# Linear attention and a two-layer sine network: longer runs of q, the key decay moved to v, two more DMA transposes, smaller filler matmuls and a new scheduler

## The chip, the cores and the metric

The kernel runs on one core of one Trainium2 chip. The metric is the device time in microseconds. Of a core's five engines, TensorE (PE) multiplies matrices into the eight banks of PSUM, VectorE (DVE), ScalarE (ACT) and GpSimd (POOL) work on vectors, and SyncE (SP) issues transfers. Each engine executes its own instructions in order; semaphores order the engines among each other.

## The reference

Inputs are q, k and v of 4 batches, 8 heads, 768 tokens and 64 channels, one decay `lam` per head, and the network's weights, all float32.

```python
for b in range(nb):                      # blocks of 64 tokens
    intra = einsum('bhic,bhjc->bhij', qb, kb) * Dmask     # lam ** (i - j) for i >= j
    intra = einsum('bhij,bhjd->bhid', intra, vb)
    inter = einsum('bhid,bhde->bhie', qb * lam ** (pos + 1), kv_state)
    out[:, :, sl] = intra + inter
    kv_state = lam ** 64 * kv_state + einsum('bhsd,bhse->bhde', kb * lam ** (63 - pos), vb)
x = out as (3072 tokens, 512)
h = x @ w_in                             # 512 -> 2048
g = h + sin(alpha * h) ** 2 / (alpha + 1e-9)
return g @ w_out                         # 2048 -> 512
```

Because the decay is a power, it splits: q of token i is multiplied by lam to the i, and something of token j by lam to the minus j; the mask is then only zeros and ones.

## The kernel before

**Tiles.** The kernel uses blocks of 128 tokens: 24 blocks, six per batch. Four blocks make a chunk of 512 tokens, the unit in which the network works; there are six chunks. A block takes these steps. Its q, k and v are loaded (`load_q` for two blocks at once, `load_kv`), 256 KB each of k and v and 512 KB of q for two blocks. `scale_block` multiplies q by its decay (L464, on POOL, one instruction per half of the heads), k by the inverse decay (L471, on POOL, for blocks 0 and 1 on DVE), both to bf16, and casts v to bf16 (L473, on ACT, from block 12 on ACT or POOL). `piece_Q` and `piece_T` transpose q and k on PE (L506, L488) and copy them out of PSUM (L511, L493); from block `TD` = 12 on `piece_T` issues one DMA transpose on SP instead (L479). `part_S` multiplies k and q to scores (L543) and masks them on DVE (L552). `part_Z` adds the block's k and v to the running state (L568), copied out at L583 (`Zc`) or, from block `SD` = 12 on, at L578 (`Zd`). `part_O` multiplies state and q (L616, or L603) and masked scores and v (L623) and copies the sum to `xT` (L632).

**The network.** A first-layer unit, `unit_A`, makes 128 of the 2048 columns for a chunk: four matmuls of 512 columns (L671), the sine on ACT (L681), its square on POOL or ACT (L686, or L685 when it is on ACT), and on DVE the sum to `gT` (L688). `unit_A2` makes 256 columns for half a chunk with eight matmuls of 256 columns (L705, L715, L719 or L720, L723); it needs only two blocks of the chunk. A second-layer unit, `unit_B`, is four matmuls (L736) over a quarter of the 2048 rows for 128 tokens; after the fourth the result is copied to `osb` on ACT (L749) and stored (L751). The four `osb` buffers are used in turn.

**Transfers.** The first quarter of `w_in` is loaded by SP as float32 (`ws`) and cast on DVE (L391); the other three quarters (`load_w1`) and the four of `w_out` (`load_w2`) are loaded and cast by POOL's queue (L342 is the one line of all loads). k, v and q lie in rings of buffers, so a load also waits until the buffer's last reader is done.

**Order.** The calls to `op` record work with what it reads and writes, and a duration. `_Plan._order` then plays the work through with those durations and gives each engine a fixed order: PE and SP from lists in which PE may look 40 ahead, the other engines whatever can start first, ties by the place in the recording less a `lead`. An operation with several engines goes to the one that would finish it first. `_transfers` estimates landings; `_settle` repeats both up to eight times. Until the first unit is ready, `spin` fills waits of PE with matmuls whose result nobody reads (L829, 512 columns). The order is fixed when the program is built: on the chip an engine waits for its next instruction even if a later one could run.

A q load of blocks 0 to 3 takes, for each partition and head, two tokens (512 bytes):

```python
for lo, hi in ((0, 4), (4, H)) if s < 4 else ((0, H),):
    ... q[b, lo:hi, n * BL:(n + 2) * BL, :].rearrange("h (p t) d -> p h (t d)", t=2)
```

Of the kernel before, what the change touches and what calls it, by code (L numbers as in the profile page):

```python
# [13 lines left out]
class _Op:  # L14


    def __init__(self, eng, emit, dur, reads, writes, dma, after, issue, lat, runs=64):
        self.eng, self.emit, self.dur = eng, emit, dur
        self.given = eng
        self.issue, self.lat, self.runs = issue, lat, runs  # L20
        self.lead = 0
# [11 lines left out]
class _Plan:  # L33

    AHEAD = {"PE": 40, "SP": 1}
    SLACK = 0.3  # L40
    EARLY = 0.0, 0.0

    LAT = 0.2
# [10 lines left out]
    def op(self, eng, emit, dur, reads=(), writes=(), dma=None, after=(), issue=0.4, lat=2.6, runs=64):  # L54
# [14 lines left out]
        o.deps.discard(o)  # L69
        o.lead = self.lead  # L70
# [4 lines left out]
    def _transfers(order):  # L75
# [5 lines left out]
        left = {e: [[o.start + 0.8, o.runs, o.dur / o.runs, o] for o in sorted(q, key=lambda o: o.start)]  # L81
# [19 lines left out]
    def _settle(self):  # L101

        filler, lands, best = self.filler, {}, None
        for _ in range(8):
            self.filler = filler
            for o in self.ops:
                o.eng, o.start, o.done = o.given, None, None
            order = self._order(lands)
            new = self._transfers(order)
            off = sum(abs(t - o.done) for o, t in new.items())  # L110
            state = [(o, o.eng, o.start, o.done) for o in order]
            if best is None or off < best[0]:
                best = off, order, state
            lands = new
# [4 lines left out]
    def _order(self, lands):  # L119
        index = {o: i - o.lead for i, o in enumerate(self.ops)}  # L120
        left = {}
        for o in self.ops:
            left.setdefault(o.eng if isinstance(o.eng, str) else "any", []).append(o)
        fixed = {e: left.pop(e, []) for e in ("PE", "SP")}
        free = [o for e in left for o in left[e]]
        clock = {e: 0.8 for e in ("PE", "SP", "ACT", "DVE", "POOL")}
        wire = 0.0
        port = 0.0
        order = []

        def ready(o):
            t = 0.0
            for d in o.deps:
                if d.done is None:
                    return None
                t = max(t, d.done + (0.0 if d.eng == o.eng else self.LAT))
            return t

        while fixed["PE"] or fixed["SP"] or free:
            best = None  # L140
            for e in ("PE", "SP"):
                can = []
                for o in fixed[e][:self.AHEAD[e]]:
# [9 lines left out]
            for o in free:  # L153
                r = ready(o)
                if r is None:
                    continue
# [773 lines left out]
```

## Time and profile before

| | us |
|---|---|
| median of three runs (lowest, highest) | 223.09 (222.61, 224.41) |
| the profiled execution | 223.52 |
| its span, first to last instruction | 221.4 |
| start of the first layer (first L705) | 19.89 |
| start of the unit that needs the second quarter of `w_in` | 23.72 |
| end of the stretch in which first and second layer alternate | 204 |

| stretch, us | PE busy | DVE | ACT | POOL | GB/s |
|---|---|---|---|---|---|
| 0 to 20 | 14.36 | 13.83 | 10.26 | 12.43 | 219 |
| 20 to 52 | 29.52 | 17.64 | 20.35 | 17.37 | 214 |
| 52 to 86 | 31.97 | 25.95 | 28.18 | 25.73 | 235 |
| 86 to 204 | 117.93 | 63.85 | 93.37 | 32.48 | 108 |
| 204 to 222 | 14.82 | 1.29 | 3.78 | 1.04 | 74 |

Busy is the time in which an engine executes an instruction; issuing a transfer and waiting count as idle. Matmuls overlap, so a single one shows 0.37 us where four in a row take 0.86. The landing of a transfer is the last of its sixteen semaphore counts.

### The profile page before, as it was taken

Reading aid. Unit: us, or ns where it says so; the run is one execution under the profiler, and the core shown is the slowest. Engines: PE = TensorE matmul, PEld = TensorE weight load, DVE = VectorE, ACT = ScalarE, POOL = GpSimd, SP = SyncE. Lnnn points to the kernel's source line nnn. Section 1 sums busy time; section 2 is a strip of 40 time slices with the busy share of each in tenths; the row PEclk is TensorE's granted clock in tenths of the full one; section 3 lists DMA queues with packets and bytes.
Section 4 is the critical chain, followed back from the end, with each engine's and each line's share of the span. In section 5 each row is a group of like instructions: output and inputs, shape, how many; then the busy total and the mean of one; then the engine's idle time right before and its main releaser. Section 6 shows DMA issues by size and latency. Waiting matters only on the chain.

```text
span 221.4 us, 4062 instructions
## 1 busy us (share of the span) xinstructions
PE 208.6 (94%) x1645; PEld 110.7 (50%) x1645; DVE 122.6 (55%) x184; ACT 155.9 (70%) x277; POOL 89.1 (40%) x100
## 2 busy tenths in 40 slices
PE   3889987899898999999999999999999999999995
PEld 1446433456575785545445444545545444444444
DVE  4687775354777887667655455645465544445100
ACT  3735994347697997788788887877788677778211
POOL 4386763454978776863576103011001011110100
DMA  5999999999999999999999752110110011101112
GB/s 131 236 232 271 206 214 208 217 235 237 233 245 275 242 191 245 219 254 189 276 240 245 155 112 33 47 50 0 47 50 21 26 47 50 47 0 49 75 70 95
DMA packets 83651, 33.31 MB, mean 150 GB/s; under 512 B 63520, under 2 KB 80688, under 8 KB 83632
## 3 DMA queue, kind: packets, MB, share of 16 engines
q1 hardware_dynamic: 76880, 24.25, 53.6%
q0 software_dynamic: 3696, 3.67, 9.9%
q10 hardware_dynamic: 3056, 5.13, 6.4%
q8 instruction: 13, 0.21, 0.4%
q14 instruction: 6, 0.05, 0.1%
HBM read 27.28 MB, written 6.29 MB: 152 GB/s over the span
## 4 chain that ended last, share of the span: by engine, by line
PE 63%; DMA 24%; POOL 4%; SPq 4%; ACT 2%; DVE 1%; issue 1%
PE bank L736 32%; PE bank L671 24%; DMA k<-in_k_dram 10%; DMA q<-in_q_dram 5%; DMA v<-in_v_dram 4%; DMA w<-in_moe_w_in_dram 4%; SPq L342 4%; PE bank L705 3%; PE bank L623 2%; PE bank L543 2%; POOL qk L471 1%; POOL qk L464 1%; PE bank L603 1%; POOL u L720 1%; DVE gT L723 1%
## 5 line engine op out<-in xcount | busy, mean ns | idle before, releaser
L736 PE MATMUL bank<-w,gT 128*128 128x512 bf16 (+1 forms) x400 | 94.8, 371 | 0.0
L688 DVE SCALAR_TENSOR_TENSOR gT<-u,rinv,bank 128x512 bf16<-128x512 bf16 x74 | 54.6, 746 | 51.7 <-ACT u L685 34.2
L671 PE MATMUL bank<-xT,w 128*128 128x512 bf16 x296 | 74.2, 379 | 0.6 <-DVE gT L688 0.6
L681 ACT ACTIVATE t<-bank,alpha 128x512 bf16<-128x512 f32 x74 | 50.6, 686 | 24.1 <-PE bank L671 24.0
L736 PEld LDWEIGHTS bank<-w,gT 128*128 128x128 bf16 x400 | 37.7, 98 | 39.6
L686 POOL TENSOR_TENSOR u<-t 128x512 bf16<-128x512 bf16 x19 | 19.7, 1040 | 80.7 <-ACT t L681 79.7
L671 PEld LDWEIGHTS bank<-xT,w 128*128 128x128 bf16 x296 | 28.5, 98 | 34.9 <-DVE gT L688 1.1
L685 ACT ACTIVATE u<-t 128x512 bf16<-128x512 bf16 x55 | 34.4, 629 | 1.8 <-DVE gT L723 0.3
L552 DVE TENSOR_TENSOR Sm<-bank,mask 128x1024 bf16<-128x1024 f32 x24 | 29.2, 1222 | 10.3 <-PE bank L568 7.7
L464 POOL TENSOR_TENSOR qk<-q,Lq 128x512 bf16<-128x512 f32 x24 | 24.5, 1044 | 21.7 <-DMA q<-in_q_dram 18.1
L471 POOL TENSOR_TENSOR qk<-k,Lk 128x512 bf16<-128x512 f32 x22 | 22.9, 1044 | 7.2 <-DMA k<-in_k_dram 7.0
L749 ACT COPY osb<-bank 128x512 f32<-128x512 f32 (+1 forms) x25 | 14.2, 569 | 14.8 <-PE bank L736 14.8
L705 PE MATMUL bank<-xT,w 128*128 128x256 bf16 x176 | 22.3, 273 | 2.0 <-DVE gT L723 2.0
L723 DVE SCALAR_TENSOR_TENSOR gT<-u,rinv,bank 128x256 bf16<-128x256 bf16 x44 | 19.1, 476 | 7.2 <-POOL u L720 4.1
L715 ACT ACTIVATE t<-bank,alpha 128x256 bf16<-128x256 f32 x44 | 18.5, 471 | 3.3 <-PE bank L705 3.1
L705 PEld LDWEIGHTS bank<-xT,w 128*128 128x128 bf16 x176 | 16.2, 98 | 5.5 <-DVE gT L723 3.0
L473 ACT CAST v<-v 128x512 bf16<-128x512 f32 x18 | 11.0, 615 | 7.6 <-DMA v<-in_v_dram 7.6
L632 ACT CAST xT<-bank 128x512 bf16<-128x512 f32 (+1 forms) x18 | 12.9, 716 | 2.8 <-PE bank L568 1.6
L720 POOL TENSOR_TENSOR u<-t 128x512 bf16<-128x512 bf16 x11 | 11.3, 1039 | 4.7 <-ACT t L715 4.6
L543 PE MATMUL bank<-qkT 64*128 64x128 bf16 x192 | 9.8, 226 | 0.2 <-DVE qkT L493 0.2
L623 PE MATMUL bank<-Sm,v 128*64 128x128 bf16 x192 | 9.9, 225 | 0.0
L829 PE MATMUL bank<-mask,ident 128*128 128x512 bf16 x12 | 5.7, 564 | 3.7 <-DVE mask L429 3.7
(55 smaller groups left out, 111.4 us busy)
## 6 DMA issues: line engine op xcount, KB each, us to landing
k<-in_k_dram SPq DMA_DIRECT2D x24, 256.0 KB, 5.5
v<-in_v_dram SPq DMA_DIRECT2D x24, 256.0 KB, 5.5
q<-in_q_dram SPq DMA_DIRECT2D x10, 512.0 KB, 5.5
out_dram<-osb ACTq DMA_DIRECT2D x19, 256.0 KB, 2.0
w<-in_moe_w_out_dram POOLq DMA_DIRECT2D x4, 512.0 KB, 13.1
w<-in_moe_w_in_dram POOLq DMA_DIRECT2D x3, 512.0 KB, 9.0
q<-in_q_dram SPq DMA_DIRECT2D x4, 256.0 KB, 4.6
ws<-in_moe_w_in_dram SPq DMA_DIRECT2D x2, 512.0 KB, 5.4
```

The lines of the kernel that those rows point to most:

```text
L464: lambda e, a=a: e.tensor_tensor(qk2[:, j:j + 2, 4 * a:4 * a + 4, :], q32[jq][:, 4 * a:4 * a + 4, :, :].rearrange("p h t d -> p t h d"), b ...
L471: lambda e: e.tensor_tensor(qk2[:, j, H:2 * H, :], k32[jl][:, :, :], lk, ALU.mult), 0.7 if s in (0,1) else 1.05,
L552: op("DVE", lambda e: e.tensor_tensor(Sm[s % 2][:, :, :], banks[:, 512 * b0:512 * b0 + 1024].rearrange("p (c i) -> p c i", i=128), mask[:, ...
L671: ins = e.matmul(ps[hb][:, c0:c1], w1[:, kc, 128 * m:128 * (m + 1)], xT[x][:, kc, c0:c1], start=(kc == 0 and c0 == lo), stop=(kc == NKC - ...
L681: op("ACT", lambda e: e.activation(t16[ju][:, w], ps[hb][:, w], ACTF.Sin, scale=alpha[:, m:m + 1]), 0.69 * f, [bank(hb), "alpha"], [("t16" ...
L685: lambda e: (e.activation(u16[ju][:, w], t16[ju][:, w], ACTF.Square) if e is nc.scalar else e.tensor_tensor(u16[ju][:, w], t16[ju][:, w], ...
L686: e.tensor_tensor(u16[ju][:, w], t16[ju][:, w], t16[ju][:, w], ALU.mult)), 0,
L688: op("DVE", lambda e: e.scalar_tensor_tensor(out=gT[g][:, m, w], in0=u16[ju][:, w], scalar=rinv[:, m:m + 1], in1=ps[hb][:, w], op0=ALU.mul ...
L705: ins = e.matmul(ps[hb][:, 256 * i:256 * i + 256], w1[:, kc, 128 * (m + i):128 * (m + i + 1)], xT[x][:, kc, lo:lo + 256], start=(kc == 0 a ...
L715: op("ACT", lambda e, i=i: e.activation(t16[ju][:, 256 * i:256 * i + 256], ps[hb][:, 256 * i:256 * i + 256], ACTF.Sin, scale=alpha[:, m + ...
L723: op("DVE", lambda e, i=i: e.scalar_tensor_tensor(out=gT[g][:, m + i, lo:lo + 256], in0=u16[ju][:, 256 * i:256 * i + 256], scalar=rinv[:, ...
L736: ins = e.matmul(ps[ob][:, w], gT[g][:, m, 128 * s4:128 * (s4 + 1)], w2[:, m, w], start=(m == 0), stop=(m == NM - 1),)
```

## The change

- q of blocks 0 to 3 is loaded in two transfers of 512 KB, each four heads of 512 tokens, in runs of four tokens (1 KB). A block of scores then takes its 128 queries from four transposed tiles with 32 columns each, and a mask of its own; `queries` gives the tiles. q of these blocks is scaled on DVE, in four instructions. The decay table gets four more rows.
- The inverse decay is multiplied into v (POOL, L524) and k is only cast (ACT, from block 12 on ACT or POOL, L521).
- `TD` goes from 12 to 10: blocks 10 and 11 are transposed by DMA.
- The fillers multiply a tile of ones, `idle`, and have 256 columns; they need only that tile.
- The mask is one 128x128 tile read eight times, instead of a 128x1024 tile; there are two, one for blocks 0 to 3.
- The loads of `w_in` and `w_out` wait for v of block 2 instead of k of block 3; the second quarter of `w_in` has a lead of 400. `prep` loads two blocks ahead from block 8 instead of 10. Chunk 0's stores are recorded after `prep(13)`.
- The scheduler: for each engine the candidates within a window of the soonest are taken by priority; the time between two dependent operations is by engine; most durations change; and `MOVES` shifts the priority of listed stretches of the recording. Engines that have a choice can choose otherwise, and every engine's order differs.

In the built programs POOL has 15 squares for 30, ACT 81 for 66; PE has 80 single transposes for 96 and 68 fillers for 12; SP has 14 DMA transposes for 12.

```diff
-    AHEAD = {"PE": 40, "SP": 1}
-    SLACK = 0.3
-    LAT = 0.2
+    AHEAD = 40
+    WINDOW = {"PE": 0.3, "ACT": 0.1, "DVE": 0.1, "POOL": 0.1}
+    PIPE = {"ACT": 0.11, "DVE": 0.09, "POOL": 0.045, "PE": 0.0}
+    HOP = {"PE": 0.055, "ACT": 0.035, "DVE": 0.035, "POOL": 0.075, "SP": 0.1}
+    DRAIN = 0.085
+    MOVES = (
+        (501, 30, "all", 10), (454, 30, "all", -180), (471, 1, "all", 140), (439, 10, "all", -70),
...
+        prio = {o: i - o.lead for i, o in enumerate(self.ops)}
+        for at, width, kind, by in self.MOVES:
+            for o in self.ops[at:at + width]:
+                if (kind == "all" and o.given != "SP") or o.given == kind or (kind == "any" and not isinstance(o.given, str)):
+                    prio[o] += by
...
+                soon = min(x[0] for x in c) + self.WINDOW.get(e, 0.0)
+                x = min((x for x in c if x[0] <= soon), key=lambda x: (x[1], num[x[2]]))
...
-    TD = 12
+    TD = 10
...
+                if s < 4:
+                    for a in range(2):
+                        last["q32", s] = load(
+                            q32[:, a, :, :, :].rearrange("p (h x) t d -> p h (x t d)", x=2),
+                            q[0, 4 * a:4 * a + 4, 0:4 * BL, :].rearrange("h (p t) d -> p h (t d)", t=4),
...
-                ported(op("DVE" if s in (0,1) else "POOL",
-                   lambda e: e.tensor_tensor(qk2[:, j, H:2 * H, :], k32[jl][:, :, :], lk, ALU.mult), 0.7 if s in (0,1) else 1.05,
-                   [("k32", jl), "Lk"], [("k2", j)]))
-                op((("ACT", 0.62, 0.0), ("POOL", 1.05, 0.3)) if s > 11 else "ACT", lambda e: (e.copy if e is nc.scalar else e.tensor_copy)(v2[j][:, :, :], v32[jl][:, :, :]), 0.62,
-                   [("v32", jl)], [("v2", j)])
+                op((("ACT", 0.62, 0.0), ("POOL", 0.62, 0.3)) if s > 11 else "ACT", lambda e: (e.copy if e is nc.scalar else e.tensor_copy)(
+                    qk2[:, j, H:2 * H, :], k32[jl][:, :, :]), 0.62, [("k32", jl)], [("k2", j)])
+                ported(op("POOL",
+                   lambda e: e.tensor_tensor(v2[j][:, :, :], v32[jl][:, :, :], lk, ALU.mult), 1.05,
+                   [("v32", jl), "Lk"], [("v2", j)]))
...
+            def queries(s):
+                nq = 4 if s < 4 else 2
+                w = BL // nq
+                return s % RT // nq * nq, nq, slice(w * (s % nq), w * (s % nq) + w)
...
-                    for ahead in range(s + 2, min(s + 3, NBLK)) if s >= 10 else ():
+                    for ahead in range(s + 2, min(s + 3, NBLK)) if s >= 8 else ():
...
             for i in range(1, 4):
-                load_w1(i, [last["k32", 3]])
+                P.lead = 400 if i <= 1 else 0
+                load_w1(i, [last["v32", 2]])
...
-                    ins = e.matmul(ps[0][:, :], ident[:, :], mask[:, 0:4, :].rearrange("p a b -> p (a b)"))
+                    ins = e.matmul(ps[0][:, 0:256], idle[:, 0:128], idle[:, :])
...
-            load_pair(10)
...
-            for st in stores:
-                if st is not None:
-                    st("SP")
             pieces = pieces_of(8, None, False) + pieces_of(10, 9, False)
...
             prep(12)
             prep(13)
+            for st in stores:
+                if st is not None:
+                    st("SP")
```

## The prediction

> **What bounds the kernel now.** I read first the page's busy shares and its costliest groups, then the waits of TensorE after 20 us, the stage table, the timelines of TensorE and ScalarE around each idle time, and the DMA issues with their landings.
>
> ```profile
> PE 208.6 (94%) x1645; PEld 110.7 (50%) x1645; DVE 122.6 (55%) x184; ACT 155.9 (70%) x277; POOL 89.1 (40%) x100
> L736 PE MATMUL bank<-w,gT 128*128 128x512 bf16 (+1 forms) x400 | 94.8, 371 | 0.0
> ```
>
> The line under the shares is the second layer; TensorE is the bound. From 19.89 us, when the first L705 starts, to 218.86, when the last result is copied out, TensorE stands still 4.5 us. Its own waits in that stretch:
>
> ```profile
> PE bank L705 <- DVE gT L723: 2.0, 3, 1.0
> PE bank L506 <- POOL qk L464: 1.7, 1, 1.7
> PE bank L671 <- DVE gT L688: 0.6, 1, 0.6
> PE bank L488 <- POOL qk L471: 0.2, 1, 0.2
> ```
>
> (total us, times, longest.) In the timeline they lie at 30.5 (0.57), 39.3 (1.72), 43.6 (0.18), 59.3 (0.82), 69.1 (1.01) and 85.4 (0.19); after 86 there is nothing to win but work itself. A unit of four 512-column matmuls takes 0.86 us there, full rate.
>
> What stands behind the idle times is mostly memory traffic:
>
> ```profile
> 17.00:19.00 2.00, 1.83 (x34) 1.00 1.11 344
> 21.00:29.00 8.00, 8.00 (x49) 1.00 1.24 206
> 30.00:36.00 6.00, 5.49 (x26) 1.00 1.19 217
> ```
>
> (stretch, length, TensorE busy, clock, DMA share, GB/s.) The DMA engines are full from 4 to 42 us. q of blocks 4 and 5 is issued at 25.87, lands 12.3 us later at 38.1, and TensorE waits for its scaling until 39.3. The wait at 59.3 is another kind:
>
> ```profile
> 54.65 0.82 ACT L715 ACTIVATE t<-bank,alpha 128x256 bf16<-128x256 f32 x2
> 57.16 0.62 ACT L473 CAST v<-v 128x512 bf16<-128x512 f32 x1 [1.69 <-DMA v<-in_v_dram]
> 57.68 0.63 ACT L719 ACTIVATE u<-t 128x512 bf16<-128x512 bf16 x1
> ```
>
> ScalarE executes in order; its cast of v waits 1.69 us for a landing, the square behind it comes late, and TensorE finds no free bank for 0.82.
>
> **The head.** Blocks 0 to 3 load q, k, v in 256 KB pieces. k and v pieces land 1.17 us apart (7.11, 8.29, 9.46, 10.62), q pieces 0.90 to 0.95 (512-byte packets), so 1 MB of q costs about 3.7. The 512 KB pieces of w (1 KB packets) land 1.40 apart (18.71 and 20.11). With q in 1 KB runs, 1 MB costs 2.8 to 3.1. The first pieces fall in the ramp (100 to 140 KB per us until 4 us), where I take nothing: for the second half that is 1.85 for 1.4 to 1.55, so 0.3 to 0.9 in all, 0.5 taken. All later landings move up so much: k of block 3 from 14.86 to 14.35, v of block 2 from 16.08 to 15.55, the w pieces from 18.71 and 20.11 to 18.2 and 19.6.
>
> The row is 287 GB/s at 10 to 11 us, 512-byte packets, against 344 at 17 to 19, 1 KB packets. The Trainium skill ("DMA: Bandwidth & Descriptors", Specifications) puts line rate at 512 bytes and up; by it the longer runs give nothing, the landings stay, and the sum below would be 0.5 smaller. The trace disagrees.
>
> From k3 the path was: scaling on POOL 1.04, transposes, copy 0.42, scores 0.33, mask 1.18, output, w cast 0.68, first layer at 19.89. Now ScalarE casts k (0.62) and may do the copy (0.59): 14.35+0.62+0.25+0.59+0.33 = 16.2, two hops of 0.1, mask until 17.6. The w cast then waits for its landing at 18.2, and the first layer starts at about 19.0, 0.9 earlier. v is scaled on POOL (1.04 for 0.62), which has the path's slack: v3 lands 16.7; behind v2 and a weight issue of 0.94 it is ready at about 18.3.
>
> But TensorE then needs quarter 1 of w_in. It issued at 15.91 and landed at 23.30; the fifth unit began at 23.72, just covered. In the changed order it is issued on v2's landing, about 15.55, and k of block 4 is issued before it without a wait, so 256 KB run beside it. Queues share by packet: at 30 to 36 us the packet records have 137 KB per us of weights (1 KB, 96 ns each) beside 70 of q (512 bytes), two to one. Beside 256-byte packets (24 ns) they get 96/(96+24) = 80% of 201, so 512 KB take 3.2 us instead of 2.55: landing 23.3 + 0.65 - 0.4 to -0.6 = 23.4. TensorE would be there at 19.0+3.83 = 22.85: it stands about 0.5, and of the 0.9 there is 0.3 left (bounds -0.3 and +0.9). The fillers are 68 of 256 columns for 12 of 512; a run too long delays the step behind it by at most nine times 0.11, and the 0.5 covers that.
>
> **20 to 52 us.** The changed TensorE order has seven second-layer units ahead of the q transposes of block 4, where there were four. From 23.4: nine units 7.8, a bank wait as before (ScalarE takes two more squares of 0.63 in this layer; 0.5 to 1.0, 0.8 taken), then ten more units (8.6) and 0.3 for quarter 2 of w_out (due about 39.0): 40.9. q, issued when quarter 2 of w_in lands (26.5 for 25.87), is there at about 38.8, its two scalings end at 40.9: no wait worth naming. k of block 4 is long there, k5 (44.0 for 44.20) too. So idle 1.1 for 2.5: 1.4 gained (0.4 to 2.0).
>
> **52 to 86 us.** Here idle is 2.0, with ScalarE busy 28.2 of 34. k lands 1.0 to 1.2 before v of the same block (56.15 and 57.14), and it is k that ScalarE now waits for; v's wait moves to POOL. Against that ScalarE takes over squares: 81 of them for 66, 9.5 us in all, some of it here. I take half of the 2.0: 1.0 (-1.0 to 2.0).
>
> **Transposes of blocks 10 and 11.** On TensorE they were 0.45 for q and two of 0.23: 0.9 off the bound, and 0.69+2*0.42 of copies. On SP they add two issues of 2 to 3 us (L479 rows: 2.73, 2.35), in front of the loads of block 14 and of chunk 0's four stores, which move behind block 13's transpose: loads of 12 and 13 from 62.0 (5.8, as now), two transposes (5.1), then what took 72.0 to 83.2, at most 11.2: stores at 81.5 to 84.1 instead of 62.6, landed 4.0 later, at 85.5 to 88.1. ScalarE's next output copy needs that buffer at about 84.5; behind it wait one sine and one square, while TensorE has four second-layer units (3.5 us) that need neither. Cover until about 88.5: nothing charged; past it each us late costs a us. The loads behind have slack: k and v of blocks 22 and 23 land by 124 us, used after 160.
>
> Masks (128x128, read with stride 0) and constants are off the path; the multiply keeps its shape, 1.22.
>
> **Sum** against the profiled execution, 223.52 (221.4 span and 2.1 around it): 0.3+1.4+1.0+0.9 = 3.6 off, 219.9. That execution is 0.43 above the median of 223.09, so 219.5.
>
> **Rivals.**
> *Landings rule all of it.* If block 4 to 11's data set the pace, only the stream's 0.5 and the transposes' 0.9 count: 1.4, 221.7. For it: a DMA share of 1.0 and more until 120 us. Against: the waits at 30.5, 59.3 and 69.1 end with VectorE. Chance 0.20.
>
> *All idle goes.* 0.9+4.5+0.9 = 6.3: 216.8. For it: no single resource is full from 52 to 86. Chance 0.08.
>
> *ScalarE's k casts, the slower side.* Nine k casts (blocks 5 to 13) stand between sines; the nine v casts waited 6.9 us in all from 20 to 86. If each cost TensorE the 0.82 of 59.3, that is 7.4 against 4.6 gained with the old idle gone: 225.9. Slower than before from six of nine, by over 1% only with all. For it: the added squares leave ScalarE less slack. Against: k lands first. Chance 0.08.
>
> *The clock falls back in the head.* Half rate shows in fillers: 0.61 us for one at 11.76, 0.38 at 15.13; TensorE needed from 3.66 to 12.3 to get fast. If the small fillers don't hold it, up to 8.6 us of first layer go at half rate, 0 to 4.3 lost; at 2, 221.5. By the Trainium skill ("TensorE: Matmul & The Clock Gate", Part 4: PE-mode transpose) transposes do not count as activity, which speaks for it; the rows from 13 to 19 us stayed fast with transposes among them. Chance 0.04.
>
> The forecast itself has 0.60 and 218.0 to 220.8. About 1% (2.2 us) is what a measurement can tell here, so bounds 220.9 and 225.3. Faster: 0.60+0.08 = 0.68; same: 0.20+0.04 and the milder k casts 0.02 = 0.26; slower 0.06. The range takes the forecast, most of the landings rival and part of the all-gone case: 217.5 to 222.5.
>
> **What will show it.** First layer at about 19.0, a wait of TensorE for the w_in DMA of about 0.5, fifth unit near 23.4; idle from there to 52 near 1.1; no wait behind a cast at 59; 40 L506 and 40 L488 transposes for 48 each; stores landing before 88. Wrong if quarter 1 lands after 24.5, if ScalarE idles over 1 us on k landings several times, or if TensorE waits after 86.

## The result, and the profile after

The changed kernel takes 225.97 us (median of 20 executions, 223.97 to 228.15), the kernel before 223.74 beside it (20, 222.61 to 225.14). The ratio is 1.0072, with a 95% interval of 1.0049 to 1.0096: a little slower, where 219.5 was predicted. Ratios, here and below, leave out executions over 1.5% above the fastest of the same kernel (four of these 20); the medians keep them. The profiled execution of after took 225.33, with a span of 223.6.

The busy shares and the costliest group of after, in the columns of before:

```profile
PE 212.9 (95%) x1685; PEld 115.1 (51%) x1685; DVE 122.2 (55%) x185; ACT 162.5 (73%) x295; POOL 72.0 (32%) x84
L795 PE MATMUL bank<-w,gT 128*128 128x512 bf16 (+1 forms) x400 | 95.3, 373 | 0.0
```

TensorE is busy 4.3 us longer than before, although 16 transposes left it. Part of that is fillers, part is real matmuls at half clock, as will be seen. Its five largest waits after 20 us (total us, times, longest):

```profile
PE bank L662 <- DVE gT L747: 2.1, 1, 2.1
PE bank L601 <- DVE gT L782: 0.9, 1, 0.9
PE bank L601 <- DMA qkT<-qk: 0.7, 1, 0.7
PE bank L764 <- ACT t L774: 0.6, 1, 0.6
PE bank L662 <- DMA qkT<-qk: 0.6, 1, 0.6
```

Of the idle times of before, the 1.72 at 39.3 is gone and the 0.57 at 30.5 is 0.41, at 31.26. One wait is new: 2.1 us in front of the matmuls of state and q (L662) of blocks 15 and 16. In TensorE's timeline of after (start, us, engine, line, operation, and in brackets the idle time before it with its releaser):

```profile
108.10 1.03 PE L795 MATMUL bank<-w,gT 128*128 128x512 bf16 x4
111.23 0.38 PE L662 MATMUL bank<-qkT,Zd 128*128 128x128 bf16 x4 [2.11 <-DVE gT L747]
112.34 1.72 PE L730 MATMUL bank<-xT,w 128*128 128x512 bf16 x4
113.85 1.91 PE L795 MATMUL bank<-w,gT 128*128 128x512 bf16 x4
```

The releaser named there, a sum on VectorE, is misleading. The group also needs the DMA transpose of block 17, since q comes in runs of two tokens for two blocks, so that the scores of block 16 read the transposed tiles of blocks 16 and 17. That transpose landed at 111.14, 0.09 us before the group starts. In before it landed at 105.94, 5.5 us ahead of the same group:

```profile
111.47 0.39 PE L603 MATMUL bank<-qkT,Zd 128*128 128x128 bf16 x4
```

In after, units of four matmuls right behind the wait take 1.7 to 1.9 us where they took 0.86 to 1.04. The stage table of after (stretch, length, TensorE busy, clock, DMA share, GB/s) has the reason:

```profile
109.00:111.00 2.00, 0.12 (x1) 1.00 0.47 94
112.00:113.00 1.00, 1.00 (x18) 0.78 1.20 319
113.00:114.00 1.00, 1.00 (x4) 0.50 1.35 228
114.00:115.00 1.00, 1.00 (x4) 0.50 1.34 217
115.00:116.00 1.00, 1.00 (x4) 0.51 1.19 225
116.00:117.00 1.00, 1.00 (x6) 1.00 1.01 230
```

After 2.11 us without matmuls the granted clock (the share of TensorE's full clock) fell to 0.50 for over three us: 112 to 116 hold 4 x 1.00 us of busy time at 0.78, 0.50, 0.50 and 0.51, which is 0.22 + 0.50 + 0.50 + 0.49 = 1.7 us of lost work. The Trainium skill ("TensorE: Matmul & The Clock Gate", Why this matters for your kernels) tells to avoid idle gaps of over about 3 us. By it this gap would have been free of that price; the measurement differs.

Why the transpose is late stands in SyncE's timeline (start, us in which it issues):

```profile
69.60 4.14 SPq L530 DMA_TRANSPOSE qkT<-qk  x2
...
83.63 2.08 SPq L810 DMA_DIRECT2D out_dram<-osb  x4
...
88.84 4.96 SPq L530 DMA_TRANSPOSE qkT<-qk  x1
95.41 1.96 SPq L530 DMA_TRANSPOSE qkT<-qk  x1
100.21 2.63 SPq L530 DMA_TRANSPOSE qkT<-qk  x1
104.13 4.73 SPq L530 DMA_TRANSPOSE qkT<-qk  x1
```

Here SyncE issues without a pause from 69.6 to 108.9. The first line is the two added transposes; the four stores of chunk 0 now follow at 83.63 instead of 62.6; the last line is block 17's, whose issue took 4.73. The casts and scalings that it reads were done at 98.45, 5.7 us before. The same one in before was issued at 101.68, in 1.91:

```profile
95.75 2.88 SPq L479 DMA_TRANSPOSE qkT<-qk  x1
101.68 1.91 SPq L479 DMA_TRANSPOSE qkT<-qk  x1
```

So its landing is 5.2 us later: 2.45 because its issue starts later and 2.8 because its issue takes longer. In before SyncE issues without a pause too, from 76.8 on, and block 17's transpose stood there 6.4 us behind its inputs (done at 95.31): the queue that got the added work was already full at that place.

### The profile page after: what moved, and what is told of

Its sections match the earlier page's. It is cut to its first block, busy times and chain, and to the rows that moved or that the text cites. A ratio compares the mean times of both kernels' runs of the same rounds, so it can differ in the third digit from the quotient of the medians.

```text
span 223.6 us, 4144 instructions
## 1 busy us (share of the span) xinstructions
PE 212.9 (95%) x1685; PEld 115.1 (51%) x1685; DVE 122.2 (55%) x185; ACT 162.5 (73%) x295; POOL 72.0 (32%) x84
## 4 chain that ended last, share of the span: by engine, by line
PE 78%; DMA 6%; DVE 5%; POOL 4%; ACT 3%; issue 2%; SPq 1%; ACTq 0%; POOLq 0%
PE bank L795 37%; PE bank L730 25%; PE bank L764 5%; DMA qkT<-qk 4%; PE bank L682 3%; PE bank L601 3%; DMA alphaT<-in_moe_alpha_dram 2%; DVE Sm L610 2%; POOL u L745 1%; PE bank L662 1%; PE bank L557 1%; DVE xT L691 1%; ACT t L774 1%; POOL u L779 1%; POOL qk L516 1%
## 5 line engine op out<-in xcount | busy, mean ns | idle before, releaser
L730 PE MATMUL bank<-xT,w 128*128 128x512 bf16 x296 | 75.0, 383 | 0.5 <-DVE gT L747 0.4
L740 ACT ACTIVATE t<-bank,alpha 128x512 bf16<-128x512 f32 x74 | 50.0, 686 | 16.7 <-PE bank L730 15.9
L744 ACT ACTIVATE u<-t 128x512 bf16<-128x512 bf16 x66 | 41.6, 630 | 2.2 <-DVE gT L782 0.2
L524 POOL TENSOR_TENSOR v<-v,Lk 128x512 bf16<-128x512 f32 x24 | 25.0, 1044 | 21.6 <-DMA v<-in_v_dram 20.2
L516 POOL TENSOR_TENSOR qk<-q,Lq 128x512 bf16<-128x512 f32 x20 | 20.5, 1044 | 20.7 <-DMA q<-in_q_dram 20.7
L521 ACT CAST qk<-k 128x512 bf16<-128x512 f32 x19 | 11.8, 620 | 2.9 <-DMA k<-in_k_dram 2.8
L890 PE MATMUL bank<-idle 128*128 128x256 bf16 x68 | 12.1, 320 | 1.3 <-DVE idle L455 1.3
L691 ACT CAST xT<-bank 128x512 bf16<-128x512 f32 (+1 forms) x16 | 11.7, 729 | 1.8 <-PE bank L682 1.2
L778 ACT ACTIVATE u<-t 128x512 bf16<-128x512 bf16 x15 | 9.5, 641 | 0.2
L779 POOL TENSOR_TENSOR u<-t 128x512 bf16<-128x512 bf16 x7 | 7.3, 1040 | 7.2 <-ACT t L774 7.2
```

What stands on the lines that cost most here:

```text
L516: lambda e, a=a: e.tensor_tensor(qk2[:, j:j + 2, 4 * a:4 * a + 4, :], q32[:, jq, 4 * a:4 * a + 4, :, :].rearrange("p h t d -> p t h d"), b ...
L524: lambda e: e.tensor_tensor(v2[j][:, :, :], v32[jl][:, :, :], lk, ALU.mult), 1.05,
L730: ins = e.matmul(ps[hb][:, c0:c1], w1[:, kc, 128 * m:128 * (m + 1)], xT[x][:, kc, c0:c1], start=(kc == 0 and c0 == lo), stop=(kc == NKC - ...
L740: op("ACT", lambda e: e.activation(t16[ju][:, w], ps[hb][:, w], ACTF.Sin, scale=alpha[:, m:m + 1]), 0.69 if hi - lo == TCH else 0.475, [ba ...
L744: lambda e: (e.activation(u16[ju][:, w], t16[ju][:, w], ACTF.Square) if e is nc.scalar else e.tensor_tensor(u16[ju][:, w], t16[ju][:, w], ...
```

## The experiments

Except where told, each kernel is after with its instruction order kept as built and only the listed edit: `_edit` runs once the planner has settled the order, `_put` moves an instruction, `at` is its planned time. Three figures compare them. *T17* is the landing of block 17's transpose (105.94 in before, 111.14 in after). *Rest* is the time from the start of the L662 group of blocks 15 and 16 to TensorE's end. *Ratio* is against runs of before on the same chip, with its 95% interval; after has 1.0072 [1.0049, 1.0096]. T17 and rest come from one profile each, and two profiles of one kernel differed by 2.1 us in T17, so a ratio weighs more than one landing. In six of the profiles the first loads landed about 2 us late; it is said where that matters.

**The stores, to ScalarE's queue.**

```diff
+    acts = [o for o in order if o.eng == "ACT"]
+    for row in range(4):
+        st = _find(order, "store", row)
+        copy = next(d for d in st.deps if d.dma is None)
+        st.eng = "ACT"
+        _put(order, st, acts[acts.index(copy) + 2], True)
```

> The four stores of chunk 0 are issued by ScalarE, each two instructions behind its copy, in place of SP between the transposes of blocks 13 and 14; every other instruction stays where it was. Queue theory (SP issues without a pause from 69.6 to 108.9 us in the changed kernel, so the 2.08 us of the stores delay all that follows): the transpose of block 14 is issued at about 86.8 in place of 88.84, that of block 17 lands at about 109 in place of 111.14, TensorE's waits of 0.55 us at 99.79 and 2.11 us at 111.23 go, and with them the stretch of half clock behind the second (1.65 us): about 4.2 us less than 225.33, ratio to before near 0.988. Order theory (TensorE's new order asks for block 16 about 9 us earlier than the old one, and the transposes wait for their own inputs): no gain, ratio near 1.007. Contention theory (the transfers themselves are slow beside the stores): the bytes stay, the wait at 111 shrinks by less than 1 us.

Ratio 1.0027 [0.9995, 1.006], 224.08 us. T17 108.58, group at 111.82: no wait for the transpose any more, but TensorE now waited 1.52 at 78.63 and 1.50 at 89.23. T17 is 2.6 us earlier without these four issues on SyncE, but freeing the queue alone gains little: the waits moved.

**The wait filled with matmuls nobody reads.**

```diff
+    g = next(o for o in order if o.eng == "PE" and any(d.tag == ("T", 17) for d in o.deps))
...
+    def spins(h):
+        for _ in range(19):
+            ins = plan.spin1(h)
+        return ins
+    f = _Op("PE", spins, 2.0, (), (), None, (), 0, 0)
...
+    order.insert(order.index(g), f)
```

> 19 unused matmuls of 128x256 are put on TensorE ahead of the group that waits for the transpose of block 17, where it stood idle for 2.11 us; nothing else moves. Clock theory (the idle stretch itself costs 1.65 us more, since the granted clock was 0.50 for the 3 us behind it): the wait stays about as long but filled, the clock stays above 0.9 from 111 to 116, and the time falls by about 1.65 us to 223.7, ratio near 1.000. If the drop comes by itself and only happens to lie there: no change, ratio near 1.007.

Ratio 1.0053 [1.0017, 1.0089], 225.14 us. Its stage table:

```profile
110.00:112.00 2.00, 2.00 (x17) 1.00 0.51 89
112.00:113.00 1.00, 1.00 (x13) 1.00 0.52 146
113.00:114.00 1.00, 0.94 (x27) 1.00 1.11 328
114.00:115.00 1.00, 0.90 (x5) 1.00 1.27 281
```

The clock holds 1.00 through the stretch that had 0.50, and 8 of 10 executions granted 0.999 or more, against 6 of 20 of after. So the half clock came from the gap. The median hardly moved (0.2% under after's ratio, inside both intervals). In the profiled execution, the slowest of the ten at 226.28 and one with late first loads, T17 landed at 112.36 and a wait of 1.05 at 133.6 appeared. What the half clock costs over all executions is therefore not shown: the six executions of after at 0.999 or more have a median of 224.40 and the other 14 one of 226.07, but the eight of this kernel at 0.999 or more have 224.6.

**The two transposes back on TensorE.** The planner ordered everything anew with this one, and the added pieces left the positions of `MOVES` where they were.

```diff
-    TD = 10
+    TD = 12
...
```

> The transposes of blocks 10 and 11 go back from SP's DMA to TensorE, as in the kernel before; the planner's moves stay on the same instructions. SP loses two transposes (4.14 us of its continuous stretch from 69.6 on), TensorE gets back 0.9 us. Queue theory: the transposes of blocks 13 to 17 are issued about 4 us earlier, so the waits of 0.66, 0.55 and 2.11 us and the 1.65 us of half clock go: 5.0 less and 0.9 more, about 221.2, ratio near 0.989. Order theory: only the 0.9 more, about 226.2, ratio near 1.011.

Ratio 1.0104 [1.0072, 1.0135], 225.78 us, T17 111.19: the figure that the theory of the order had given. It proves little: the new plan also changed the order of loads, and the first loads of the profiled execution landed late.

**Before, with blocks 10 and 11 by DMA.**

```diff
-    TD = 12
+    TD = 10
```

> The kernel before with one edit: DMA transposes from block 10 in place of block 12; its own planner makes the order. Queue theory: SP of before has pauses until 76.8 us, and blocks 14 and 16 had 3.9 and 12.5 us to spare there, so two more transposes (about 4.5 us of SP) use up the slack of block 14 and little more: TensorE gets 0.9 less work and waits at most 0.6 more, ratio between 0.996 and 1.000. If DMA transposes beside stores and loads are what is slow (contention theory), waits of over 1 us on transposes appear here too, with a stretch of half clock, and the ratio is 1.003 or more.

Ratio 1.0255 [1.0197, 1.0313], 229.9 us. The constant also sets where before's later loop begins, so this kernel does blocks 10 and 11 twice (26 scalings, 16 DMA transposes). Its time answers nothing.

**Without the two transposes.** The DMA transposes of blocks 10 and 11 are left out, so what uses them reads stale tiles.

```diff
+    drop = [o for o in order if o.tag in [("T", 10), ("T", 11)]]
+    for o in drop:
+        order.remove(o)
...
```

> The two DMA transposes of blocks 10 and 11 are left out of the changed kernel and nothing is put in their place (blocks 10 and 11 are computed from what their tiles held before); all else stays. Stream theory, which takes the place of the queue theory (the DMA engines are busy without a pause until 125 us, each transpose takes as long as a 256 KB load, 1.2 us, and TensorE, ahead of the transfers by then, waits wherever it asks next for what they bring): everything behind lands 2.4 us earlier or a little more, the waits of 0.66, 0.55 and 2.11 us shrink by about that and the 1.65 us of half clock go: 223.74 x 0.990, about 221.5. Order theory (the transposes are asked for too early, whatever is ahead of them): ratio 1.005 to 1.007.

Ratio 0.9954 [0.9921, 0.9987], 223.63 us: 1.2% below after's ratio, in spite of a new wait of 2.76 us at 131.7 (behind ScalarE's cast of k of block 23) and half clock after it. T17 109.08, and the group started right behind it, at 109.17. TensorE had come there at 107.59, 1.5 us earlier than in after, so 1.58 of the 2.11 us of wait were left, with the clock at full.

**Without the four stores** of chunk 0, which are left out.

```diff
+    drop = [o for o in order if o.tag in [("store", r) for r in range(4)]]
...
```

> The four stores of chunk 0 (1 MB of output) are left out of the changed kernel; all else stays. Moving them to ScalarE took the wait at 111 us away and brought 1.5 us at 78 and 89 us, which the stream theory explains by the same bytes passing earlier. Stream theory: 1 MB less to pass before 100 us, with 2.7 us between the first and the last landing of the four, frees about 3 us: no wait over 0.4 us after 84 us, no half clock, ratio near 0.988. ScalarE theory (in the run with the stores on ScalarE, four issues on that engine made the casts of k late): also no stores on ScalarE here, but SP's 2.08 us alone are freed: the wait at 111 goes, those at 85 and 99 stay, ratio 0.992 to 0.996. Order theory: 1.005 to 1.007.

Ratio 0.9938 [0.9902, 0.9975], 222.16 us, T17 106.73, group at 110.40, no wait; this profile is one with late first loads. Moving the stores to ScalarE's queue had gained 0.45%, leaving them out 1.3%, so their issue on SyncE is not all that they cost. Which part is their bytes and which their load on ScalarE is not separated. Each of the two omissions is worth about 1.2 to 1.3% by itself (1.0072 less 0.9954 and less 0.9938). The two T17s lie 2.1 and 4.4 us earlier than after's; the sum, 6.5, exceeds the 5.2 that T17 moved, so they are not to be added.

**Transposes 10 to 17 ahead of the loads** on SyncE.

```diff
...
+    for s, key in ((10, ("v32", 12)), (11, ("v32", 13)), (12, ("v32", 14)), (13, ("k32", 15)),
+                   (14, ("store", 0)), (15, ("v32", 16)), (16, ("q32", 18)), (17, ("v32", 18))):
+        _put(sp, _find(sp, "T", s), _find(sp, *key))
```

> In SP's queue of the changed kernel the transposes of blocks 10 to 17 are each put ahead of two to four of the transfers that stood before them (loads of q, k and v for blocks 12 to 18, and the four stores ahead of which the transpose of block 14 now stands); the other engines keep their order. In the profile of the changed kernel those of blocks 10, 13 and 14 were issued 5, 7 and 7 us after their casts and scalings were done. If the place in SP's queue is what is late: the wait at 75.89 shrinks, those at 85.65, 99.79 and 111.23 and the half clock go, about 4 us less, ratio near 0.99. Stream theory: the bytes are the same, so the loads of blocks 14 to 18 land 1 to 5 us later and their transposes with them: the waits shrink by a part only, ratio 0.998 to 1.005.

Ratio 1.0169 [1.0117, 1.0222], 227.84 us, worse than either theory had it. T17 gained 1.1 us (110.08), every load behind lost: k of block 23 landed at 133.4 (130.1 in after, 123.1 in before), the group started at 114.01 and TensorE waited 1.62 at 116.8. Late first loads (first layer at 24.00) are a part of this one profile. Over all executions too no time was won: with the queue full, its order only chose who was late.

**Chunk 0's output copies flat.** The copies write contiguously, so the rows of the chunk stay permuted, and the stores put them right.

```diff
-                        ... .rearrange("p a (x t) -> p a t x", t=nq),
+                        ... .rearrange("p a (x t) -> p a t x" if s > 3 else "p a (t x) -> p a t x", t=nq),
...
-                    op(eng, lambda e: e.dma_start(out[row:row + 128, w], osb[jo][:, w]), 0.75,
+                    op(eng, lambda e: e.dma_start(out[row:row + 128, w] if c else out[row:row + 128, w].rearrange("(x t) d -> t x d", t=4), osb[jo][:, w]), 0.75,
```

> The copies of the attention output of blocks 0 to 3 into xT lose the step of four elements (128x4x4x32 becomes 128x4x128: the tokens of a block stay in the order of the runs), and the four stores of chunk 0 put the rows back in order by their addresses in the output; all else stays. Copy theory of the head: the copies on VectorE take about 0.73 in place of 1.29 us, the first layer starts about 0.5 us sooner (the cast of w_in then waits for the landing at 18.78) and the second unit's wait of 0.56 us goes; the fifth unit still waits for its quarter of w_in (24.59). Stream theory: what the head gains is waited for later, ratio 1.004 to 1.008. If the head decides: ratio 1.001 to 1.003.

Ratio 1.0544 [1.0486, 1.0601], 235.44 us. The first of the copies in VectorE's timeline, after and then this kernel:

```profile
14.20 1.29 DVE L691 CAST xT<-bank 128x512 bf16<-128x512 f32 x1
```

```profile
14.21 0.68 DVE L691 CAST xT<-bank 128x512 bf16<-128x512 f32 x1
```

Writing in steps of four bf16 costs 1.29 for 0.68 (0.73 in steps of two, as before had it); the first layer started at 19.81 for 19.96, so little of it was on the path. What was lost is in the stores:

```profile
86.00:88.00 2.00, 2.00 (x11) 1.00 0.20 55
88.00:90.00 2.00, 1.17 (x6) 1.00 0.26 102
```

A DMA share of 0.20 to 0.26 while a permuted store runs. The Trainium skill ("DMA: Bandwidth & Descriptors", Why a DMA increments its semaphore by 16 and not by 1) says that a transfer is spread over the largest number of engines up to 16 that divides the slowest dimension of both patterns. Here that is 4 (rows of the output) and 128 (partitions of the buffer), so 4 of 16 engines, a share of 0.25, and the rows agree. Transposes queued behind: block 14's was issued at 101.18 (88.84 in after), T17 was 118.66.

**The group two units later.**

```diff
+    for s, by in ((16, 2.2),):
+        g = next(o for o in order if o.eng == "PE" and any(d.tag == ("T", s + 1) for d in o.deps))
+        for o in [g] + [o for o in order if g in o.deps and o.eng != "PE"]:
+            at[o] += by
...
```

> In the changed kernel, TensorE's group of blocks 15 and 16 (the one that waited 2.11 us for the transpose of block 17) and what VectorE and ScalarE do with its results stand two units (1.75 us) later in their queues; nothing else moves, and no transfer is touched. Order theory (TensorE was asked for this group too early; there was other work to do): the wait falls to about 0.4 us, the half clock behind it (1.65 us) goes, 3.4 us less than 225.33 in an execution like the profiled one; over all executions, of which 14 of 20 showed a clock under 0.995, 2 to 3 us, ratio 0.994 to 0.999. Stream theory: the same at this place, but the transposes of blocks 18 to 20 are next; 1 us of wait comes back behind them: ratio 0.999 to 1.003. If the clock drop comes by itself: ratio near 1.000.

Ratio 1.0084 [1.0046, 1.0123], 225.59 us. In its profile no wait at the group and no half clock, but two other waits:

```profile
114.00 1.04 PE L730 MATMUL bank<-xT,w 128*128 128x512 bf16 x4 [1.45 <-ACT xT L691]
132.81 1.04 PE L795 MATMUL bank<-w,gT 128*128 128x512 bf16 x4 [1.83 <-ACT xT L691]
```

The first is for the output of block 15, which the same group makes and which chunk 3's first unit needs: two units of delay were more than the order had to spare behind the group. The second stands in ScalarE's timeline:

```profile
130.27 0.62 ACT L521 CAST qk<-k 128x512 bf16<-128x512 f32 x1 [2.03 <-DMA k<-in_k_dram]
130.79 0.68 ACT L740 ACTIVATE t<-bank,alpha 128x512 bf16<-128x512 f32 x1
```

ScalarE stood 2.03 us at a cast of k of block 23, whose tokens are needed much later, with a sine for TensorE behind it.

**The head: no fillers, all at once, fewer.** Without fillers:

```diff
-                if i == 0:
+                if i < 0:
```

> The unused matmuls of the head are left out of the changed kernel (all 73 of them); the rest keeps its order. In some executions (three of the runs above) the first loads land about 2 us later than in the profiled run of the changed kernel; there TensorE runs out of fillers, idles 2.5 us, and the transposes of q then stand behind fillers at half speed (4 fillers 1.06 us for 0.60), with the first layer at 23.8 for 19.96. If fillers in the way cost more than the clock they keep: the first layer starts earlier in such an execution (21 to 22), ratio at or under 1.005. If the clock they keep is worth more: the first layer starts in half clock, the fifth unit 1.5 to 2 us later than 24.63, ratio 1.008 to 1.016.

Ratio 0.9985 [0.9942, 1.0029], 223.7 us. (The profile has 68 fillers; the 73 of the expectation is wrong.) Its profile is one with late first loads: the first layer began at 22.51, where four kernels with fillers and late loads began at 23.78 to 24.26. With 44 in one go, and the transpose of alpha moved behind those of q and k:

```diff
-                op("PE", lambda e: e.transpose(ps[4][:, 0:NM], alphaT[:, :], identf[0:NM, 0:NM]), 0.3,
+                op("PE", lambda e: e.transpose(ps[5][:, 0:NM], alphaT[:, :], identf[0:NM, 0:NM]), 0.3,
...
+    emit, first.emit = first.emit, lambda h: [emit(h), plan.spin1(h, 16)][1]
```

> In the head of the changed kernel 44 unused matmuls in one go replace the first 20 and the following 8, and the transpose of alpha with VectorE's three small steps on it moves behind the transposes of q and k (to another bank), so that the scaling of q waits for lam alone and no longer for alpha; all else stays. With the first loads landing early: q is scaled about 1 us sooner, the first layer still waits for the cast of w_in (19.7 to 20.0). With them landing late: TensorE stays at full clock and the first layer starts at 21 to 22 in place of 23.8. If the head decides the time in those executions: ratio 1.000 to 1.004. Stream theory: what the head gains is waited for behind 84 us: ratio 1.005 to 1.009.

Ratio 1.0088 [1.0049, 1.0127], 225.21 us, clock 0.999 or more in all ten executions, and no time won. In its profile the first layer began at 20.91, not at the 19.7 to 20.0 of the expectation, so there the head saved nothing; whether it saves time when the first loads land late, no profile of it shows. That kernel and the later group together:

```diff
+        for o in [g] + [o for o in order if g in o.deps and o.eng != "PE"]:
+            at[o] += by
...
+    emit, first.emit = first.emit, lambda h: [emit(h), plan.spin1(h, 16)][1]
```

> Both edits, the later group of blocks 15 and 16 and the longer run of unused matmuls with alpha behind q and k. If the two add up: 2 to 4 us less than the changed kernel, ratio 0.990 to 0.997, faster than the kernel before. If the head's gain is waited for at the stream, or one undoes the other: the ratio of the later group alone.

Ratio 1.0073 [1.004, 1.0106], 225.3 us, waits of 1.09 at 114.0 and 1.15 at 132.2. Only the first 28 fillers:

```diff
+    fill = [o for o in order if o.eng == "PE" and o.reads == ("idle",)]
+    for o in fill[2:]:
+        order.remove(o)
```

> Only the first 20 and the following 8 unused matmuls stay in the changed kernel, those between the transposes and behind them are left out. If they cost by standing in front of the transposes (4 of them 0.60 us at full, 1.06 us at half clock): as no_fillers, ratio 0.997 to 1.001. If the clock matters more than the place: between the two, 1.001 to 1.005. If neither and the gain of no_fillers was chance: 1.005 to 1.008.

Ratio 1.0009 [0.9972, 1.0047], 224.63 us, between the two. The clock was 0.992 or less in all ten executions; in the profile it is 0.50 from 15 to 21.8 us, with no single wait of TensorE over 1 us between 6 and 21.8. So the fillers do hold the clock in the head, and yet the kernel without these is the faster one.

**The late casts of k on GpSimd.** Those of blocks 12, 13, 15, 18, 19, 22 and 23 that the planner had given to ScalarE:

```diff
+    for s in range(12, 24):
+        t = _find(order, "T", s)
+        for d in t.deps:
+            if d.writes == (("k2", s % 6),) and d.eng == "ACT" and s >= 12:
+                d.eng = "POOL"
```

> The casts of k of blocks 12, 13, 15, 18, 19, 22 and 23 move from ScalarE to GpSimd in the changed kernel (those of 14, 16, 17, 20 and 21 are there already); ScalarE's sines no longer stand behind a load. ScalarE theory (in later_sixteen ScalarE waited 1.82 us for the load of k at 109.48 and 2.03 us at 130.27, and TensorE 1.83 us at 132.81 behind the second): 0.5 to 2 us less than the changed kernel, ratio 0.998 to 1.005. Stream theory: the transposes come no sooner, the waits at 85, 99 and 111 us stay: ratio 1.005 to 1.008. If GpSimd is late with the scaling of q and v for it (0.6 us each cast): ratio over 1.008.

Ratio 1.0035 [0.9995, 1.0076], 225.15 us; in the profile no wait after the group any more, 1.60 us of idle at the group, and the clock at full. In five of the ten executions it was 0.993 or less. The interval overlaps after's, so the gain is likely and not sure. The same, without fillers:

```diff
+                d.eng = "POOL"
...
-                if i == 0:
+                if i < 0:
```

> The same, and without the unused matmuls. If the two causes are separate and add up: no_fillers (0.9985) and what casts_on_pool gains over the changed kernel, ratio 0.990 to 0.996. If both only let the same lateness through in another place: ratio 0.997 to 1.001.

Ratio 0.9967 [0.9932, 1.0001], 222.97 us. T17 110.32 and the group at 110.41, 0.09 later:

```profile
110.41 0.38 PE L662 MATMUL bank<-qkT,Zd 128*128 128x128 bf16 x4 [0.91 <-issue]
```

With the stores on ScalarE's queue as well:

```diff
+                d.eng = "POOL"
...
-                if i == 0:
+                if i < 0:
...
+        st.eng = "ACT"
...
```

> The casts on GpSimd, no unused matmuls, and the stores of chunk 0 from ScalarE. The stores on ScalarE took 0.45% off the changed kernel with ScalarE 0.99 busy from 60 to 70 us; with fewer casts there, they should cost it less. If all add up: ratio 0.985 to 0.992. If ScalarE from 45 to 70 us is the limit (the moved casts all lie behind it): as casts_pool_no_fillers or up to 0.4% over it.

Ratio 1.0008 [0.9981, 1.0036], 224.04 us: T17 108.19, earlier, but the group only at 111.69, with TensorE at work until then. Its profile is one with late first loads (first layer at 22.80) and has a wait of 1.49 at 79.21, 0.25 behind the landing of block 11's transpose. What the stores on ScalarE have to do with it is not shown; the ratio says that the three gains do not add up.

**The best of them once more, and with alpha's transpose later.**

```diff
+                d.eng = "POOL"
...
-                if i == 0:
+                if i < 0:
```

> The kernel of casts_pool_no_fillers once more, in five rounds. If its gain is real: ratio 0.994 to 0.999, the interval under 1. If it was chance: 0.999 to 1.003.

Ratio 0.9946 [0.9912, 0.998], 222.62 us (221.09 to 224.86), below 1 over its whole interval: a version a little faster than both kernels, 0.5% under before and 1.3% under after. In its profile the transpose landed at 108.26:

```profile
107.92 1.03 PE L795 MATMUL bank<-w,gT 128*128 128x512 bf16 x4
108.79 0.39 PE L662 MATMUL bank<-qkT,Zd 128*128 128x128 bf16 x4
```

No wait is left at the group. The same program had 110.32 in its other profile, and its spans were 220.9 and 219.3.

```diff
-                op("PE", lambda e: e.transpose(ps[4][:, 0:NM], alphaT[:, :], identf[0:NM, 0:NM]), 0.3,
+                op("PE", lambda e: e.transpose(ps[5][:, 0:NM], alphaT[:, :], identf[0:NM, 0:NM]), 0.3,
...
```

> The same with the transpose of alpha and VectorE's three steps on it behind the transposes of q and k, so that q is scaled as soon as lam has landed. With the first loads landing late, q is scaled 0.9 us sooner (all_three: lam landed at 6.77, alpha at 8.06) and the first layer starts that much sooner; with them landing early, what is gained is waited for at 76 and 111 us. Stream theory: 0 to 0.5 us less than same_again, ratio 0.993 to 0.998. If the head decides: 0.9 us or more, ratio under 0.993.

Ratio 0.9963 [0.9936, 0.9991], 223.32 us: nothing more.

**Taken together.**

| kernel | T17 landed | group starts | rest | waits of TensorE behind the group |
|---|---|---|---|---|
| before | 105.94 | 111.47 | 107.35 | none |
| after | 111.14 | 111.23 | 109.74 | none, half clock |
| without_ten_eleven | 109.08 | 109.17 | 112.58 | 2.76, half clock |
| without_first_stores | 106.73 | 110.40 | 108.33 | 0.19 |
| warm_head | 110.68 | 110.77 | 109.14 | 1.01 |
| casts_on_pool | 110.81 | 110.90 | 107.96 | none |
| casts_pool_no_fillers | 110.32 | 110.41 | 107.96 | none |
| same_again | 108.26 | 108.79 | 107.97 | none |

The rest is 107.96 us, give or take 0.01, in the five kernels with these casts on GpSimd, and longer by about the waits and the half clock where there are any. In five of the eight the group starts 0.1 us after block 17's transpose. So in the profiles the time is set by when the group starts, which in after is one landing, by what TensorE waits behind it, and by the clock.

## Why the prediction was wrong

Step by step, in us taken off TensorE's end (218.82 in before, 220.97 in after):

| step | predicted | measured | from |
|---|---|---|---|
| head | 0.3 | -0.9 | fifth unit at 24.63 for 23.72 |
| 20 to 52 | 1.4 | 2.1 | idle behind that unit 0.41 for about 2.5 |
| 52 to 86 | 1.0 | 0.1 | idle 1.96 for 2.02 |
| transposes of 10 and 11 | 0.9 | 0.9 | 80 singles for 96, counted at the prediction's price |
| 86 to the group | 0 | -0.6 | a wait of 0.55 at 99.79, for block 15's transpose (landed 99.7) |
| the wait at the group | 0 | -2.1 | 2.11 |
| half clock behind it | 0 | -1.8 | 109.74 less 107.96 |

The first five sum to 1.6. Read directly, TensorE reached the group at 109.12 (111.23 less the wait) for 111.47, with 0.6 more work left behind it (107.96 for 107.35), so it led by 1.7. The wait and the half clock took 3.9 from that and left it 2.15 late.

- **The step that failed** is "nothing charged" for the transposes and stores moved on SyncE, with "The loads behind have slack". It checked the buffer of the stores (they landed by 88.85, one just past the 88 named) and the use of blocks 22 and 23 after 160, but not the nearest customers of the queue: block 15's transpose had 3.5 us of slack in before (landed 95.35, needed at 98.86) and block 17's 5.5. The latter landed 5.2 later, and TensorE, by the very gains of the sum, came to the group 2.35 earlier: 5.2 + 2.35 - 5.5 is about the wait of 2.1, and by these numbers neither alone would have made one. Leaving out the transposes or the stores brings the ratio under 1 in either case, so leaving out either one is enough to undo the loss. "After 86 there is nothing to win but work itself" was right for before, and the same sentence hid that there was something to lose.
- **The sum added past the point where it stops.** Gains ahead of a landing that is fixed by another queue are waited for again. The profiles show it from the other side: in that of spin_at_16 the first layer began 3.8 us later than in after (23.78 for 19.96), but TensorE came to the group only 1.6 later (110.68 for 109.12), since the waits of 0.87 and 0.66 at 75.89 and 85.65 were gone. A kernel with an earlier start that lost it again is not among the runs.
- **The half clock had no price**, 1.7 to 1.8 us in the profiled execution. The clock rival put it in the head, not behind a wait at 111. In the head the fillers held it up (few_fillers shows what happens without most of them).
- **The fillers** were put at nothing ("at most nine times 0.11, and the 0.5 covers that"). Leaving them all out changed the ratio from 1.0072 to 0.9985, as much as the whole loss, and leaving out those among the transposes to 1.0009. The 0.11 was the price of one at full clock; in an execution with late first loads four of them stood 1.06 us in front of each group of transposes. With late loads the first layer began 1 to 1.75 us sooner without them; with early loads it began at 20.39 to 21.41 without and 19.81 to 20.69 with all 68.
- **The head** was missed by 1.2. The first layer began at 19.96, not 19.0, and the second quarter of `w_in` landed at 24.59 for 23.4 (24.5 was named as the point of failure). The copies of 1.29 us had been overlooked, but flat ones gave only 0.15. Most of the miss is in the loads (k of block 4, issued at 15.59, was under way beside the second piece of w, which the sum did not have): the last k of blocks 0 to 3 landed at 14.59 for the 14.35 of the prediction, the first piece of w at 18.78 for 18.2, the second at 21.22 for 19.6.
- **20 to 52 us** was right in kind and 0.7 too small. No wait stands behind a cast at 59, as predicted, and 80 single transposes were left.
- **52 to 86 us**: half of the idle was to go, none did. Other waits took the place of those that left: 0.87 at 75.89, a quarter of a microsecond after block 11's added transpose had landed (75.64), and 0.66 at 85.65, as block 13's landed (85.6).
- **The rivals.** "Landings rule all of it" was right in kind; its 221.7 counted only gains. ScalarE's k casts did stop TensorE, not from 20 to 86 as thought but at about 132, and not in after: only in kernels whose wait at 111 was gone, filled or shorter.

What stays open: how much of the 5.2 us of block 17's transpose is due to the added transposes and how much to the stores, and why its issue took 4.73; whether SyncE's queue or the memory traffic is the tighter limit there; how the fillers' 0.9% comes about over all executions, and how it combines with the queue's lateness, since either alone is as large as the loss.

## What to carry to other kernels

When an edit puts transfers on an in-order queue, list the next users of every transfer behind it and their slack in the trace of before, nearest first, and stop adding gains at the first one that runs out. The time by which the other gains bring the bounding engine there sooner comes off that slack too. When TensorE starts within 0.1 us of the landing of something that it reads, take that landing for its releaser, whatever engine the wait names. A load-dependent cast belongs on an engine with no urgent work queued behind it; here moving seven of them and dropping the fillers turned 0.7% slower into 0.5% faster.

## What the runs showed of the hardware

- The length of an idle time of TensorE alone did not tell whether the clock would fall. 1.60, 1.72 and 1.83 us (casts_on_pool, transposes_first, later_sixteen) left it at full. 1.66 us in before_ten_by_dma (until 83.44) were followed by 0.50 from 84 to 87, and 2.11 (after) and 2.76 (without_ten_eleven) by 0.50 for about 3 us as well. In flat_copies two of 1.76 within five us were followed by 0.50 from 93 to 99.
- Issuing one DMA transpose on SyncE took 2 to 3 us as a rule, and 4.96 and 4.73 us twice in after. ScalarE issued a store within 1.5 us of the start of both, but it also did so in before with the transposes issued at 95.75 and 106.06, which took 2.88 and 3.00: that the stores are the cause is not shown. The landings of two in a row were 1.22 us apart (74.42 and 75.64).
- The first loads landed late in 6 of 20 profiled executions (`lam` at 6.8 to 7.0 us for 4.3 to 4.6). In that of spin_at_16 TensorE stood 2.50 us behind the first 20 fillers, as its timeline has it:

```profile
8.21 0.26 PE L485 MATMUL bank<-identf,alphaT 16*128 16x16 f32 x1 [2.50 <-DMA alphaT<-in_moe_alpha_dram]
8.40 1.89 PE L890 MATMUL bank<-idle 128*128 128x256 bf16 x8
```

The eight fillers behind that wait took 1.89 us, where after, with a wait of 0.46 at the same place, took 1.22, and those in front of the transposes ran at half rate too (four in 1.06 for 0.60). The first 20 had been at half rate already (4.45 us in both), so here the pause kept the clock from rising. In transposes_first, where TensorE stood 3.38 us, the granted clock fell to 0.50 from 8 to 14. Fillers that wait for nothing did not keep TensorE fast where an instruction between them waited for a load.
